# Fused attention and MoE on one core: the first MoE product of the last two token chunks by one level of Strassen's method, with the late attention replanned

## The chip, the core and the metric

The kernel runs on one core of one Trainium2 chip. The metric is device time in microseconds (us), the median of several runs of the whole program. The engines are TensorE (PE in the profile, PEld for its weight loads), VectorE (DVE), ScalarE (ACT), GpSimd (POOL) and SyncE (SP), which issues the DMAs. Each engine works through its own instructions in the order in which they were written, and waits on semaphores of the others.

## What is computed

Attention over q, k, v of 4 batches, 8 heads, 576 positions and 64 channels, in two parts that are added: one over the sequence averaged by 4, one over a band of seven neighbours. Its result is the input of a two-layer product with a gated activation:

```python
x = attn_out.transpose(0, 2, 1, 3).reshape(2304, 512)
h = x @ w_in                 # 2304 x 512 @ 512 x 2048
g = h * tanh(softplus(h))
out = g @ w_out              # 2304 x 2048 @ 2048 x 512
```

## The kernel before

**Precision.** TensorE works on fp32r operands, and each operand is kept as a high part (a copy rounded by ACT) and a low part (what is left, by a subtraction on DVE). Each product is three matmuls: high by high, high by low, low by high. So everything below that is multiplied exists twice, and one step is "x3" in the order.

**Tiling.** The 2304 tokens are six chunks of `CH` = 384. The 2048 hidden features are 16 tiles f of 128, the 512 channels four tiles p of 128. A slot s is one pair (chunk c, tile f): 96 slots, in the order chunks 0 and 1 interleaved, then chunks 2 to 5 one after another, 16 slots each. Slots 64 to 79 are chunk 4 and slots 80 to 95 chunk 5.

**A slot** (`slot`, L578 to L645) first makes h, transposed, as a 128x384 tile in a PSUM bank: four channel tiles by three matmuls of 384 columns, 12 matmuls (L591). Then comes the activation (L600 to L619): ACT exp (L605), DVE clamp and add (L606), ACT square, log and exp (L608, L609, L611), DVE product with h (L612, into the buffer mH), ACT copy of the high part (L615) and DVE low part (L617), both into g. Then g is multiplied by w_out: three blocks i of 128 tokens by three matmuls of 512 columns, 9 matmuls (L630), which add up over the 16 tiles f in three PSUM banks acc. After the chunk's last f, acc is copied out by ACT and DVE (L639, L642) and stored by SP (L645).

**Buffers.** PSUM has eight banks: two for h, three for acc of the current chunk, three (`att1`) for attention, which acc of chunk 1 borrows. In SBUF the buffers that matter here are mA (3), mH (2), g (2), stg (3 staging buffers of 128x1024, also for the outputs) and x (one tag for each channel tile, 3 buffers).

**Order.** Nothing runs in the order of the source. `op` records an instruction group with its engine, a cost, its buffers and a priority; `Plan.order` (L148) then plays the engines forward in time with the costs and latencies written in the file, and on each engine issues next what is ready and has the lowest priority number. That order is what the program gets; buffers of a tag are handed out in the order in which they were recorded. Priorities are slot numbers: a slot's first product has s, its activation s + 0.2, its second product s plus an entry of `LAG`, and attention of batch b and head pair p has `ATT[b][0] + ATT[b][1] * p + UNIT[b, p]`. Attention of batches 2 and 3 is spread between slots of chunks 2 and 3 this way, since chunk 4 needs batches 2 and 3, and chunk 5 batch 3.

Of the kernel before, what the change touches and what calls it, by code (L numbers as in the profile page):

```python
# [296 lines left out]
class Kernel:  # L297
# [48 lines left out]
    def attention(self, b, p, sb, ps, padded, loose):  # L346
# [25 lines left out]
        pc3 = lambda: pc()[:, :3 * C].rearrange("p (m c) -> p m c", m=3)  # L372
        cst, A = buf("cst", [P, 4, 3]), buf("A", [P, 3, C])
        cs = 2.0 ** -7
# [200 lines left out]
            self.w[nm, f] = w  # L575


    def slot(self, s, c, f):  # L578
# [20 lines left out]

        for c0, c1, key in parts:  # L600
            n, o_ = c1 - c0, slice(c0, c1)
            pl.prio = s + 0.2
# [9 lines left out]
            op("dve", dve(n), lambda o_=o_: nc.vector.scalar_tensor_tensor(  # L612
                out=H()[:, o_], in0=A()[:, o_], scalar=0.5, in1=h()[:, o_], op0=ALU.subtract, op1=ALU.mult),
               r=[h_, a_], w=[x_], two=False)
            op("act", act(n), lambda o_=o_: nc.scalar.activation(g()[:, 0, o_], H()[:, o_], AF.Copy, scale=-2.0),  # L615
               r=[x_], w=[one])
            op("dve", dve(n), lambda o_=o_: nc.vector.scalar_tensor_tensor(  # L617
                out=g()[:, 1, o_], in0=H()[:, o_], scalar=-2.0, in1=g()[:, 0, o_].bitcast(F32),
                op0=ALU.mult, op1=ALU.subtract), r=[x_, one], w=[two])  # L619
        wo = self.w["wo", f]  # L620
        if first:
            where, tag = ("attps", "att1") if c == 1 else ("moeps", None)
            self.acc[c] = [pl.buf(where, tag or f"acc{i}", [P, 512], F32, self.nb[where, tag] if tag else 1, f"acc{s}_{i}")
                           for i in range(3)]
        for i in range(3):
            a_ = self.acc[c][i]

            def mm2(i=i, a_=a_):
# [8 lines left out]
            o = pl.buf("stg", "stg", [P, 1024], F32, self.nstg, f"o{c}_{i}")  # L637
            if i % 2:
                op("dve", dve(512), lambda a_=a_, o=o: nc.vector.tensor_copy(o()[:, :512], a_()),  # L639
                   r=[a_], w=[o], prio=s + 1, two=False)  # L640
# [4 lines left out]
            op("sp", P * 2048 / RATE, lambda r0=r0, o=o: nc.sync.dma_start(self.out[r0:r0 + P, :], o()[:, :512]), r=[o], prio=s + 1)  # L645

    def run(self, ctx):
        tc = self.tc
# [42 lines left out]
        todo = [(c, f) for _, c, f in both] + [(c, f) for c in range(2, 6) for f in range(self.NF)]  # L691
# [94 lines left out]
```

## Time and profile before

| | |
|---|---|
| median of 3 runs | 526.4 us (525.13 to 528.31) |
| the profiled execution, its time | 523.15 us |
| its span in the trace | 521.4 us |
| PE busy | 504.4 us, 97% of the span, 4862 matmuls |
| ACT busy, DVE busy, POOL busy | 360.6, 299.0, 41.0 us |
| chain of waits | PE 73%, DVE 9%, ACT 7%, DMA 7% |

The span is the time from the first to the last instruction that the trace shows; what lies around it is 1.75 us in the profiled execution. Busy times are the time in which at least one instruction of the engine was under way, from its start to its end, so an engine whose instructions overlap at their ends is counted once. In the trace an instruction's duration is longer than its spacing from the next, where they follow each other without a wait.

### The profile page before, as it was taken

To read this page: it belongs to the slowest core of one execution; us is meant where nothing else is said; L and a number is where in the kernel's file an instruction comes from. 1 tells how busy PE (TensorE), PEld (TensorE's weight loads), DVE (VectorE), ACT (ScalarE), POOL (GpSimd) and SP (SyncE) were. 2 spreads that over 40 slices of the span, in tenths; PEclk is the share of its full clock that TensorE was granted. 3 is DMA by queue.
4 is the path that set the end of the run, shared out by engine and by line. 5 is a ranking of instruction groups with operands and counts; after the bars stand their busy time and mean duration, and the time that the engine had idled before them with its cause. 6 is when DMAs were issued, how large, how long until landed. Compare 5 with 4: busy or idle time off the path is not lost.

```text
span 521.4 us, 11714 instructions
## 1 busy us (share of the span) xinstructions
PE 504.4 (97%) x4862; PEld 432.5 (83%) x4862; DVE 299.0 (57%) x669; ACT 360.6 (69%) x872; POOL 41.0 (8%) x62
## 2 busy tenths in 40 slices
PE   8779989899999999999999999999999999999997
PEld 4556679798888999888888898899888989898885
DVE  5758999788884234576776745833333333334242
ACT  3668898899996567666666667666667565665753
POOL 6420112000000000001111110100000000000000
PEclk9979999999999999999999999999999999999999
DMA  8963476444530001233323313200001000010001
GB/s 345 411 235 117 142 263 215 161 161 159 206 123 0 1 0 62 107 126 122 116 97 138 127 61 108 93 1 1 1 0 62 0 1 1 1 61 1 0 1 60
DMA packets 11861, 50.66 MB, mean 97 GB/s; under 512 B 1312, under 2 KB 1312, under 8 KB 9760
## 3 DMA queue, kind: packets, MB, share of 16 engines
q1 hardware_dynamic: 11808, 49.91, 26.4%
q8 instruction: 38, 0.62, 0.5%
q14 instruction: 15, 0.12, 0.1%
HBM read 45.19 MB, written 4.72 MB: 96 GB/s over the span
## 4 chain that ended last, share of the span: by engine, by line
PE 73%; DVE 9%; ACT 7%; DMA 7%; issue 2%; SPq 0%; DVEq 0%
PE acc L630 31%; PE h L591 31%; DMA qk<-in_qk_dram 4%; DMA stg_wi<-in_w_in_dram 3%; PE sc L380 2%; PE sl L419 2%; PE pve L506 2%; DVE g L617 1%; DVE mH L612 1%; PE pvo L506 1%; PE pt L491 1%; DVE wo L573 1%; ACT mA L608 1%; PE warm L717 1%; ACT mA L609 1%
## 5 line engine op out<-in xcount | busy, mean ns | idle before, releaser
L591 PE MATMUL h<-x,wi 128*128 128x384 f32 x1152 | 226.0, 340 | 2.0 <-DVE mH L612 1.8
L630 PE MATMUL acc<-wo,g 128*128 128x512 f32 x864 | 219.0, 394 | 0.0
L591 PEld LDWEIGHTS h<-x,wi 128*128 128x128 f32 x1152 | 200.6, 188 | 17.5 <-DVE mH L612 9.5
L630 PEld LDWEIGHTS acc<-wo,g 128*128 128x128 f32 x864 | 159.8, 188 | 27.0 <-issue 0.2
L617 DVE SCALAR_TENSOR_TENSOR g<-mH,g 128x384 fp32r<-128x384 f32 (+1 forms) x98 | 55.5, 568 | 56.0 <-ACT g L615 55.5
L605 ACT ACTIVATE mA<-h 128x384 f32<-128x384 f32 (+1 forms) x98 | 47.0, 482 | 56.1 <-PE h L591 55.9
L612 DVE SCALAR_TENSOR_TENSOR mH<-mA,h 128x384 f32<-128x384 f32 (+1 forms) x98 | 53.1, 543 | 47.3 <-ACT mA L611 45.3
L606 DVE TENSOR_SCALAR mA<-mA 128x384 f32<-128x384 f32 (+1 forms) x98 | 34.9, 359 | 69.5 <-ACT mA L605 69.1
L615 ACT ACTIVATE g<-mH 128x384 fp32r<-128x384 f32 (+1 forms) x98 | 50.3, 515 | 25.3 <-PE acc L630 24.4
L608 ACT ACTIVATE mA<-mA 128x384 f32<-128x384 f32 (+1 forms) x98 | 50.5, 517 | 24.5 <-DVE mA L606 23.8
L609 ACT ACTIVATE mA<-mA,one 128x384 f32<-128x384 f32 (+1 forms) x98 | 59.5, 608 | 2.4
L611 ACT ACTIVATE mA<-mA 128x384 f32<-128x384 f32 (+1 forms) x98 | 49.9, 510 | 1.1
L452 POOL TENSOR_TENSOR vv<-vv 128x512 f32<-128x512 f32 x16 | 22.1, 1380 | 293.6 <-DMA vv<-in_vv_dram 293.6
L365 DVE TENSOR_REDUCE qkd<-qk 128x288 f32<-128x1152 f32 x16 | 21.5, 1346 | 11.3 <-DMA qk<-in_qk_dram 11.3
L506 PEld LDWEIGHTS pve<-PT,vv 38*64 38x64 f32 x640 | 20.8, 136 | 7.8 <-issue 4.5
L506 PE MATMUL pve<-PT,vv 38*64 38x32 f32 x640 | 22.8, 221 | 3.1 <-issue 3.0
L387 ACT ACTIVATE A<-sc,cst 128x144 f32<-128x144 f32 x48 | 17.9, 377 | 5.8 <-DVE cst L385 5.0
L419 PEld LDWEIGHTS sl<-qk 64*32 64x32 f32 x1152 | 12.4, 107 | 9.5 <-issue 6.5
L717 PE MATMUL warm<-ident 128*128 128x512 bf16 x61 | 18.6, 434 | 1.6 <-POOL ident masks.py:199 1.6
L419 PE MATMUL sl<-qk 64*32 64x38 f32 x1152 | 14.8, 198 | 4.1 <-issue 3.0
L531 ACT ACTIVATE x<-x 128x384 fp32r<-128x384 f32 (+1 forms) x32 | 12.8, 441 | 8.4 <-DVE x L519 8.0
L506 PE MATMUL pvo<-PT,vv 38*64 38x32 f32 x512 | 18.4, 222 | 0.2 <-ACT xd L486 0.2
(80 smaller groups left out, 421.7 us busy)
## 6 DMA issues: line engine op xcount, KB each, us to landing
vv<-in_vv_dram SPq DMA_DIRECT2D x16, 1152.0 KB, 5.3
qk<-in_qk_dram SPq DMA_DIRECT2D x16, 582.0 KB, 5.7
stg_wi<-in_w_in_dram SPq DMA_DIRECT2D x16, 512.0 KB, 4.1
stg_wo<-in_w_out_dram SPq DMA_DIRECT2D x16, 512.0 KB, 3.7
out_dram<-o SPq DMA_DIRECT2D x18, 256.0 KB, 2.0
```

The costliest lines, as they stand in the source:

```text
L419: nc.tensor.matmul(sl3()[64 * h + 32 * f:64 * h + 32 * f + 32, t], qk()[r_, 0, k0 + 3:k0 + 35], qk()[r_, 1, k0:k0 + KW], start=not pmask, ...
L506: nc.tensor.matmul(o_()[64 * h:64 * h + 64, c0:c0 + 32], vw()[64 * e:64 * e + KW, t // 2, f, 64 * h:64 * h + 64], PT()[64 * e:64 * e + KW, ...
L591: nc.tensor.matmul(h()[:, :CH], w()[:, a, kt * P:(kt + 1) * P], x()[:, b_, :], start=kt == 0 and j == 0, stop=kt == 3 and j == 2)
L605: op("act", act(n, True), lambda o_=o_: nc.scalar.activation(A()[:, o_], h()[:, o_], AF.Exp), r=[h_], w=[a_])
L606: op("dve", dve(n, True), lambda o_=o_: nc.vector.tensor_scalar(A()[:, o_], A()[:, o_], float(math.exp(20.0)), 1.0, op0=ALU.min, op1=ALU.a ...
L608: op("act", act(n), lambda o_=o_: nc.scalar.activation(A()[:, o_], A()[:, o_], AF.Square), w=[a_])
L609: op("act", act(n, False, 1), lambda o_=o_: nc.scalar.activation(A()[:, o_], A()[:, o_], AF.Ln, bias=self.one), w=[a_])
L611: op("act", act(n), lambda o_=o_: nc.scalar.activation(A()[:, o_], A()[:, o_], AF.Exp, scale=-1.0), w=[a_])
L612: op("dve", dve(n), lambda o_=o_: nc.vector.scalar_tensor_tensor(out=H()[:, o_], in0=A()[:, o_], scalar=0.5, in1=h()[:, o_], op0=ALU.subtr ...
L615: op("act", act(n), lambda o_=o_: nc.scalar.activation(g()[:, 0, o_], H()[:, o_], AF.Copy, scale=-2.0), r=[x_], w=[one])
L617: op("dve", dve(n), lambda o_=o_: nc.vector.scalar_tensor_tensor(out=g()[:, 1, o_], in0=H()[:, o_], scalar=-2.0, in1=g()[:, 0, o_].bitcast ...
L630: nc.tensor.matmul(a_(), g()[:, a, i * P:(i + 1) * P], wo()[:, b_], start=first and j == 0, stop=last and j == 2)
```

## The change

Chunks 4 and 5 are taken together, two f tiles at a time: a quartet of four slots (two chunks by two tiles). Their four products h are seen as a 2 by 2 matrix product of blocks: x split by channel halves (tiles 0 and 1, tiles 2 and 3) and by chunk, w_in by channel halves and by the two f tiles. Strassen's method in Winograd's form needs seven block products in place of eight. A block product is two channel tiles by three matmuls, so a quartet takes 42 matmuls of 384 columns in place of 48. The second products stay as they are.

- `prepare` makes the sums of x (S1 to S4, each for two channel tiles, with high and low parts) once, with priority 42. They lie in buffers that attention no longer uses (`vv`, `qk`), in x buffers, and work in the three stg buffers.
- `blocks` makes the sums of w_in (T1 to T4) for each pair of f tiles: 12 DVE instructions and 4 ACT copies of 128x256.
- `quartet` issues the products into the two h banks. One ACT copy takes the first product out of PSUM, and seven DVE additions (`plus`) combine the others into the four h tiles, now in SBUF; each tile then goes through the same activation (`tail`, the second half of the old `slot`).
- acc of chunk 5 takes the three attention banks, so both chunks add up at once. Outputs of chunk 4 go to x buffers, and outputs i = 0 and 1 of the other chunks share one stg buffer.
- `LAG` for the late slots is 9.95, was 7.07. `ATT` and `UNIT` of batches 2 and 3 change. Up to slot 47 the order of PE is the same as before.

```diff
-LAG = (7.26, 4.32, 7.07)
+LAG = (7.26, 4.32, 9.95)
...
-ATT = {0: (-817.1, 44.0), 1: (-77.2, 21.6), 2: (-43.4, 22.6), 3: (27.0, 12.1)}
+ATT = {0: (-817.1, 44.0), 1: (-77.2, 21.6), 2: (-49.7, 24.2), 3: (31.9, 8.4)}
...
+    def prepare(self):
...
+        pl.prio = SPRE
+        for j in range(2):
+            for k, x in (("a22", X(j + 2, 5)), ("a21", X(j, 5)), ("a11", X(j, 4)), ("a12", X(j + 2, 4))):
+                b, i, v = at(k, j)
+                op("dve", dve(W), lambda v=v, x=x: nc.vector.tensor_tensor(
+                    out=v(), in0=x()[:, 0].bitcast(F32), in1=x()[:, 1].bitcast(F32), op=ALU.add), r=[x], w=[(b, i)])
+            mix("a22", "a21", "a22", j, ALU.add)
+            mix("a21", "a11", "a21", j, ALU.subtract)
+            mix("a11", "a22", "a11", j, ALU.subtract)
+            mix("a12", "a12", "a11", j, ALU.subtract)
+            for k, t in (("a22", 1), ("a11", 2), ("a21", 3)):
+                split(k, j, t)
+        for j in range(2):
+            split("a12", j, 4)
...
+    def quartet(self, s, i):
...
+        def product(k, w, x):
+            bank = pl.buf("moeps", "h", [P, 512], F32, 2, f"h{k}_{s}")
+            wb_, wv = w
+            for j in range(2):
+                xb, key, xv = x[j]
+
+                def mm(j=j, xv=xv):
+                    for m, (a, b_) in enumerate(((0, 0), (0, 1), (1, 0))):
+                        nc.tensor.matmul(bank()[:, :CH], wv(a, j), xv()[:, b_], start=j == 0 and m == 0, stop=j == 1 and m == 2)
...
+        def plus(to, a, bank):
+            op("dve", dve(CH), lambda: nc.vector.tensor_tensor(
+                out=at[to](), in0=bank()[:, :CH], in1=at[a](), op=ALU.add),
+               r=[bank] + u[a] * (a != to), w=u[to], prio=s + UPRE, two=False)
+
+        bank = product(0, wt(w0, 0), xs(0, 4))
+        op("act", act(CH, True), lambda bank=bank: nc.scalar.activation(at["u1"](), bank()[:, :CH], AF.Copy),
+           r=[bank], w=u["u1"], prio=s + UPRE)
+        plus("u2", "u1", product(1, tt(2), ss(2)))
+        plus("u1", "u1", product(2, wt(w0, 2), xs(2, 4)))
+        self.tail(s, 4, 2 * i, u["u1"], at["u1"])
+        plus("u3", "u2", product(3, tt(3), ss(3)))
+        bank = product(4, tt(1), ss(1))
+        plus("u4", "u3", bank)
+        self.tail(s + 1, 5, 2 * i + 1, u["u4"], at["u4"], ("x", "x2"), False)
+        plus("u2", "u2", bank)
+        plus("u3", "u3", product(5, tt(4), xs(2, 5)))
+        self.tail(s + 2, 5, 2 * i, u["u3"], at["u3"], last=2 * i + 2 == self.NF)
+        plus("u2", "u2", product(6, wt(w1, 2), ss(4)))
+        self.tail(s + 3, 4, 2 * i + 1, u["u2"], at["u2"], ("x", "x3"))
...
-            where, tag = ("attps", "att1") if c == 1 else ("moeps", None)
+            where, tag = ("attps", "att1") if c in (1, 5) else ("moeps", None)
...
-        slots(todo[32:])
+        slots(todo[32:48])
+        self.prepare()
+        slots(todo[48:])
+        for i in range(self.NF // 2):
+            self.quartet(s, i)
+            s += 4
```

How the instructions move, at three places. In the names, h89 is the product of slot 89, h2_84 is block product 2 of the quartet that begins with slot 84, acc64 and acc65 are the sums of chunks 4 and 5, t2 and sfar are sums of w_in and x, and x3 at the end is a step's three matmuls.

PE, two slots late in the run, before (the rows of two slots, then the next acc):

```order
L591 MATMUL h89_5797<-x0_5_4058,wi9_1951 128x384 x3
L591 MATMUL h89_5797<-x1_5_4125,wi9_1951 128x384 x3
L591 MATMUL h89_5797<-x2_5_4524,wi9_1951 128x384 x3
L591 MATMUL h89_5797<-x3_5_4917,wi9_1951 128x384 x3
L591 MATMUL h90_5815<-x0_5_4058,wi10_2037 128x384 x3
L591 MATMUL h90_5815<-x1_5_4125,wi10_2037 128x384 x3
L591 MATMUL h90_5815<-x2_5_4524,wi10_2037 128x384 x3
L591 MATMUL h90_5815<-x3_5_4917,wi10_2037 128x384 x3
L630 MATMUL acc80_0_5642<-wo5_1728,g85_5785 128x512 x3
```

The same place in the quartet of slots 84 to 87, after:

```order
L678 MATMUL h2_84_5841<-x2_4_3517,wi10_2037 128x384 x3
L678 MATMUL h2_84_5841<-x3_4_3734,wi10_2037 128x384 x3
L678 MATMUL h3_84_5851<-x0_5_4056,t3_5_5706 128x384 x3
L678 MATMUL h3_84_5851<-x1_5_4123,t3_5_5706 128x384 x3
L678 MATMUL h4_84_5861<-sfar_4861,t1_5_5720 128x384 x6
L678 MATMUL h5_84_5873<-x2_5_4387,t4_5_5741 128x384 x3
L678 MATMUL h5_84_5873<-x3_5_4892,t4_5_5741 128x384 x3
L769 MATMUL acc65_0_5269<-wo6_1804,g78_5765 128x512 x3
L678 MATMUL h6_84_5896<-s4_0_5008,wi11_2077 128x384 x3
L769 MATMUL acc65_1_5304<-wo6_1804,g78_5765 128x512 x3
L769 MATMUL acc65_2_5313<-wo6_1804,g78_5765 128x512 x3
L678 MATMUL h6_84_5896<-s4_1_5013,wi11_2077 128x384 x3
```

A product that was 12 matmuls is now 6, four products follow each other without other work between them, and each still takes one of two banks.

DVE, what two slots issued before, in full:

```order
L606 TENSOR_SCALAR mA89_5819<-mA89_5819 128x384
L606 TENSOR_SCALAR mA90_5836<-mA90_5836 128x384
L617 SCALAR_TENSOR_TENSOR g87_5851<-mH87_5792,g87_5851 128x384
L612 SCALAR_TENSOR_TENSOR mH89_5858<-mA89_5819,h89_5797 128x384
L617 SCALAR_TENSOR_TENSOR g88_5867<-mH88_5810,g88_5867 128x384
L612 SCALAR_TENSOR_TENSOR mH90_5876<-mA90_5836,h90_5815 128x384
```

The first 11 of the 31 that a quartet issues now:

```order
L755 SCALAR_TENSOR_TENSOR g80_5828<-u1_80_5674,g80_5828 128x384
L685 TENSOR_TENSOR u23_84_5839<-h1_84_5792,u1_84_5834 128x384
L755 SCALAR_TENSOR_TENSOR g81_5845<-u4_80_5718,g81_5845 128x384
L685 TENSOR_TENSOR u1_84_5834<-h2_84_5841,u1_84_5834 128x384
L685 TENSOR_TENSOR u23_84_5839<-h3_84_5851,u23_84_5839 128x384
L744 TENSOR_SCALAR mA84_5859<-mA84_5859 128x384
L650 TENSOR_TENSOR t3_6_5866<-b12_6_5725,t3_6_5866 128x256
L685 TENSOR_TENSOR u4_84_5878<-h4_84_5861,u23_84_5839 128x384
L640 TENSOR_TENSOR b12_7_5885<-wi15_2323 128x256
L685 TENSOR_TENSOR u23_84_5839<-h4_84_5861,u23_84_5839 128x384
L685 TENSOR_TENSOR u23_84_5839<-h5_84_5873,u23_84_5839 128x384
```

The additions that free the banks stand between the sums of w_in for the next quartets and the activations of this one.

The entry into the first quartet: DVE before, at the end of chunk 3, and after.

```order
L617 SCALAR_TENSOR_TENSOR g63_5035<-mH63_4974,g63_5035 128x384
L612 SCALAR_TENSOR_TENSOR mH65_5042<-mA65_5003,h65_4980 128x384
L617 SCALAR_TENSOR_TENSOR g64_5051<-mH64_4994,g64_5051 128x384
L612 SCALAR_TENSOR_TENSOR mH66_5060<-mA66_5020,h66_4999 128x384
L606 TENSOR_SCALAR mA67_5069<-mA67_5069 128x384
L606 TENSOR_SCALAR mA68_5086<-mA68_5086 128x384
L639 COPY o3_1_5099<-acc48_1_4291 128x512
```

```order
L750 SCALAR_TENSOR_TENSOR mH63_5048<-mA63_5024,h63_4998 128x384
L755 SCALAR_TENSOR_TENSOR g63_5059<-mH63_5048,g63_5059 128x384
L650 TENSOR_TENSOR t2_1_5069<-b22_1_4973,t2_1_5069 128x256
L640 TENSOR_TENSOR b22_2_5075<-wi5_1710 128x256
L782 COPY o3_0_5092<-acc48_1_4480 128x512
L685 TENSOR_TENSOR u23_64_5101<-h1_64_5055,u1_64_5050 128x384
L685 TENSOR_TENSOR u1_64_5050<-h2_64_5065,u1_64_5050 128x384
```

PE there, after:

```order
L769 MATMUL acc48_0_4470<-wo15_2356,g63_5059 128x512 x3
L769 MATMUL acc48_1_4480<-wo15_2356,g63_5059 128x512 x3
L769 MATMUL acc48_2_4487<-wo15_2356,g63_5059 128x512 x3
L678 MATMUL h3_64_5105<-x0_5_4056,t3_0_4918 128x384 x3
L678 MATMUL h3_64_5105<-x1_5_4123,t3_0_4918 128x384 x3
```

The copy of the finished acc of chunk 3 now stands on DVE ahead of the addition that frees the bank which h3_64 needs.

## Rows read from the trace of the kernel before

**Rows 1.** The page, parts 1 and 2: PE busy, and its clock in 40 slices.
```profile
PE 504.4 (97%) x4862; PEld 432.5 (83%) x4862; DVE 299.0 (57%) x669; ACT 360.6 (69%) x872; POOL 41.0 (8%) x62
PEclk9979999999999999999999999999999999999999
```

**Rows 2.** The chain of waits in 425 to 446 us: start, duration, what.
```profile
430.13 4.21 PE h L591 x24
434.34 4.12 PE acc L630 x18
```

**Rows 3.** Stages: window, its length, busy time (instructions) of PE, PEld, DVE, ACT, POOL; clock.
```profile
60.00:120.00 60.00, 57.09 (x517) 50.10 (x516) 53.60 (x114) 53.13 (x120) 4.77 (x4) 1.00 0.55 185
240.00:320.00 80.00, 79.30 (x1064) 68.39 (x1063) 52.02 (x125) 55.24 (x147) 11.07 (x10) 1.00 0.32 115
320.00:390.00 70.00, 70.00 (x642) 62.15 (x642) 33.13 (x74) 45.56 (x100) 2.27 (x2) 1.00 0.08 27
390.00:507.00 117.00, 117.00 (x592) 105.07 (x591) 42.76 (x87) 73.16 (x144) 0.00 (x0) 1.00 0.04 14
```

**Rows 4.** What PE waited for in 60 to 120 us: us in total, times, longest.
```profile
PE h L591 <- DVE mH L612: 1.5, 2, 1.3
```

**Rows 5.** Groups by line and shape, 390 to 507 us: busy, mean ns; idle before.
```profile
L609 ACT ACTIVATE mA<-mA,one 128x384 f32<-128x384 f32 x28 | 17.2, 616 | 0.8
L612 DVE SCALAR_TENSOR_TENSOR mH<-mA,h 128x384 f32<-128x384 f32 x29 | 16.0, 553 | 1.0
L617 DVE SCALAR_TENSOR_TENSOR g<-mH,g 128x384 fp32r<-128x384 f32 x28 | 15.7, 559 | 33.3 <-ACT g L615 33.0
L608 ACT ACTIVATE mA<-mA 128x384 f32<-128x384 f32 x28 | 14.7, 525 | 6.2 <-DVE mA L606 6.0
L605 ACT ACTIVATE mA<-h 128x384 f32<-128x384 f32 x28 | 13.8, 492 | 23.9 <-PE h L591 23.9
L606 DVE TENSOR_SCALAR mA<-mA 128x384 f32<-128x384 f32 x28 | 10.1, 360 | 38.9 <-ACT mA L605 38.9
```

**Rows 6.** Groups of DVE by line and shape, whole run.
```profile
L519 DVE TENSOR_TENSOR x<-pvo,xd 128x256 f32<-128x256 f32 x16 | 6.6, 415 | 0.0
L639 DVE COPY o<-acc 128x512 f32<-128x512 f32 x6 | 4.2, 692 | 4.9 <-PE acc L630 4.9
```

**Rows 7.** Timeline of DVE at 69 and 103 us: start, duration, instruction.
```profile
69.10 0.41 DVE L519 TENSOR_TENSOR x<-pvo,xd 128x256 f32<-128x256 f32 x1
69.43 0.55 DVE L617 SCALAR_TENSOR_TENSOR g<-mH,g 128x384 fp32r<-128x384 f32 x1
...
102.73 0.35 DVE L606 TENSOR_SCALAR mA<-mA 128x384 f32<-128x384 f32 x1
103.00 0.55 DVE L617 SCALAR_TENSOR_TENSOR g<-mH,g 128x384 fp32r<-128x384 f32 x1
103.46 0.55 DVE L612 SCALAR_TENSOR_TENSOR mH<-mA,h 128x384 f32<-128x384 f32 x1
```

**Rows 8.** Timeline of PE while DVE is at its busiest.
```profile
87.31 4.35 PE L591 MATMUL h<-x,wi 128*128 128x384 f32 x24
91.51 4.28 PE L630 MATMUL acc<-wo,g 128*128 128x512 f32 x18
...
104.07 2.37 PE L591 MATMUL h<-x,wi 128*128 128x384 f32 x12 [1.33 <-DVE mH L612]
```

**Rows 9.** Timeline of all engines, 432 to 434 us.
```profile
432.30 0.49 ACT L605 ACTIVATE mA<-h 128x384 f32<-128x384 f32 x1 [1.60 <-PE h L591]
432.82 0.36 DVE L606 TENSOR_SCALAR mA<-mA 128x384 f32<-128x384 f32 x1 [0.95 <-ACT mA L605]
433.22 0.53 ACT L608 ACTIVATE mA<-mA 128x384 f32<-128x384 f32 x1 [0.43 <-DVE mA L606]
```

**Rows 10.** Timeline, the end of the run.
```profile
507.17 10.40 PE L630 MATMUL acc<-wo,g 128*128 128x512 f32 x45
517.61 0.60 ACT L642 ACTIVATE o<-acc 128x512 f32<-128x512 f32 x1 [0.76 <-PE acc L630]
```

More of the change, by code (lines that the diff above doesn't have):

```diff
@@ L41 @@
 TAIL = 0
+SPRE = 42
+TPRE = -2
+UPRE = -2
 TICK, BUSY, PACE = 3413.3, 3060, 1.6
@@ new lines, in blocks @@
+    def blocks(self, i):
+        nc, pl = self.nc, self.plan
+        op, n = pl.op, 256
+        w0, w1 = self.w["wi", 2 * i], self.w["wi", 2 * i + 1]
+        t = {k: pl.buf("att", tag, [P, n], F32, 1, f"{k}_{i}")
+             for k, tag in (("b11", "A"), ("b12", "AT"), ("b21", "vd"), ("b22", "qkd"))}
+        for k, w, c in (("b11", w0, 0), ("b12", w1, 0), ("b22", w1, n), ("b21", w0, n)):
+            op("dve", dve(n), lambda k=k, w=w, c=c: nc.vector.tensor_tensor(
+                out=t[k](), in0=w()[:, 0, c:c + n].bitcast(F32), in1=w()[:, 1, c:c + n].bitcast(F32), op=ALU.add),
+               r=[w], w=[t[k]])
+        T = {}
+        for j, (ko, a, b_, place) in ((1, ("b11", "b12", "b11", ("att", "L"))), (3, ("b12", "b22", "b12", ("att", "x32"))),
+                                      (2, ("b22", "b22", "b11", ("att", "PT"))), (4, ("b21", "b21", "b22", ("stg", "tmp")))):
+            op("dve", dve(n), lambda ko=ko, a=a, b_=b_: nc.vector.tensor_tensor(
+                out=t[ko](), in0=t[a](), in1=t[b_](), op=ALU.subtract), r=[t[a], t[b_]], w=[t[ko]])
+            T[j] = w = pl.buf(*place, [P, 2, n], F32R, 1, f"t{j}_{i}")
+            op("act", act(n), lambda w=w, ko=ko: nc.scalar.activation(w()[:, 0], t[ko](), AF.Copy), r=[t[ko]], w=[(w, 0)])
+            op("dve", dve(n), lambda w=w, ko=ko: nc.vector.tensor_tensor(
+                out=w()[:, 1], in0=t[ko](), in1=w()[:, 0].bitcast(F32), op=ALU.subtract), r=[t[ko], (w, 0)], w=[(w, 1)])
+        return T
@@ L594, in slot, with tail @@
             op("pe", 527, mm, r=[w, x], w=[h], cols=1152, prio=s + 0.1 * kt / 4)
-        A = pl.buf("mish", "mA", [P, CH], F32, NMISH[0], f"mA{s}")
-        H = pl.buf("mish", "mH", [P, CH], F32, NMISH[1], f"mH{s}")
-        g = pl.buf("mish", "g", [P, 2, CH], F32R, 2, f"g{s}")
+        self.tail(s, c, f, h)
+    def tail(self, s, c, f, h, own=None, place=("mish", "g"), last=None):
+        nc, pl = self.nc, self.plan
+        op = pl.op
+        last = f == self.NF - 1 if last is None else last
+        A = pl.buf("mish", "mA", [P, CH], F32, NMISH[0], f"mA{s}")
+        psum = own is None
+        if psum:
+            Hv, own = pl.buf("mish", "mH", [P, CH], F32, NMISH[1], f"mH{s}"), h
+            h, H = [[(b, m) for m in range(3)] for b in (h, Hv)]
+        else:
+            Hv, H = own, h
+        g = pl.buf(*place, [P, 2, CH], F32R, 3 if place[0] == "x" else 2, f"g{s}")
         parts = [(0, CH, None)] if s < 95 - TAIL else [(i * P, (i + 1) * P, i) for i in range(3)]
@@ L612, in slot @@
             op("dve", dve(n), lambda o_=o_: nc.vector.scalar_tensor_tensor(
[L613 to L616, printed above, removed]
+                out=Hv()[:, o_], in0=A()[:, o_], scalar=0.5, in1=own()[:, o_], op0=ALU.subtract, op1=ALU.mult),
+               r=[*h_, a_], w=x_, two=not psum)
+            op("act", act(n), lambda o_=o_: nc.scalar.activation(g()[:, 0, o_], Hv()[:, o_], AF.Copy, scale=-2.0),
+               r=x_, w=[one])
             op("dve", dve(n), lambda o_=o_: nc.vector.scalar_tensor_tensor(
-                out=g()[:, 1, o_], in0=H()[:, o_], scalar=-2.0, in1=g()[:, 0, o_].bitcast(F32),
-                op0=ALU.mult, op1=ALU.subtract), r=[x_, one], w=[two])
+                out=g()[:, 1, o_], in0=Hv()[:, o_], scalar=-2.0, in1=g()[:, 0, o_].bitcast(F32),
+                op0=ALU.mult, op1=ALU.subtract), r=[*x_, one], w=[two])
         wo = self.w["wo", f]
+        first = c not in self.acc
         if first:
-            where, tag = ("attps", "att1") if c == 1 else ("moeps", None)
+            where, tag = ("attps", "att1") if c in (1, 5) else ("moeps", None)
             self.acc[c] = [pl.buf(where, tag or f"acc{i}", [P, 512], F32, self.nb[where, tag] if tag else 1, f"acc{s}_{i}")
@@ L626, in slot, with mm2 @@
             a_ = self.acc[c][i]
-            def mm2(i=i, a_=a_):
+            def mm2(i=i, a_=a_, first=first, last=last):
                 for j, (a, b_) in enumerate(((0, 0), (0, 1), (1, 0))):
@@ L690, in run @@
         both = sorted([(f, 0, f) for f in range(self.NF)] + [(f + LEAD + 0.5, 1, f) for f in range(self.NF)])
-        todo = [(c, f) for _, c, f in both] + [(c, f) for c in range(2, 6) for f in range(self.NF)]
+        todo = [(c, f) for _, c, f in both] + [(c, f) for c in range(2, 4) for f in range(self.NF)]
         s = 0
```

71 lines of the change are left out of this document (61 added, 10 removed).

## The prediction

> **What bounds the kernel now.** I read the page first, then the chain of waits, then stages in a table of windows, and then single spacings. The page has PE busy for 97% of the span at full granted clock after the first slices [rows 1], and busy PE can still hide gaps, so the chain decides. In the last stage it is PE alone: 24 matmuls of the first product, then 18 of the second, and so on, with no other engine between them [rows 2]. That gives two prices: 4.21 / 24 = 0.1754 us for a matmul of 384 columns, 4.12 / 18 = 0.2289 us for one of 512. The stages show the same: from 320 us on PE is never idle, with DVE at 47% and then 37% and ACT at 65% and 63%; only early, with DVE busy 53.6 of 60 us, does PE lose 2.9 us [rows 3]. So in slots 64 to 95 the time is the number of matmuls, and the other engines have room. The question is how much of that room the change uses up.
>
> **What is removed.** Eight quartets lose 6 matmuls each of 384 columns: 48 x 0.1754 = 8.4 us, all on the chain. The order shows six matmuls for each product in place of twelve, and seven products. The price holds when DVE is busy: at 87 us, where DVE is at 89%, 24 matmuls take 91.51 - 87.31 = 4.20 us [rows 3, 8]. (The Trainium skill, "TensorE: Matmul & The Clock Gate", Back-to-back issue gap, gives columns / 2.4 + 2.5 ns, 162.5 ns here, by which the gain would be 7.8 us. The trace disagrees, with 175.4 ns, and the trace is used.)
>
> **What is added, quartet by quartet.** PE needs 42 x 0.1754 + 36 x 0.2289 = 15.6 us for a quartet, before it was 16.7. DVE issues 31 instructions: seven additions and eight activation steps of 384 elements, four clamps, 12 sums of 256. Where they follow each other the spacing is 0.46, 0.27 and 0.33 us [rows 7], so 15 x 0.46 + 4 x 0.27 + 12 x 0.33 = 12.0 us, 77% of 15.6. An addition from PSUM is priced as L612, which reads PSUM and SBUF too [rows 5]. ACT has four times five activations (four at 0.525, the log at 0.616), one copy from PSUM at 0.492 and four copies of 256, for which 0.525 is an upper bound: at most 13.5 us, 86% [rows 5]. Neither is full, so the sums of w_in and x cost nothing by themselves; they are hidden behind PE. What counts is whether PE waits for them in turn. Three waits are new in each quartet.
>
> First, a bank. A product lasts 6 x 0.1754 = 1.05 us, and the one after the next needs its bank. The release takes the step from PE to the reader, one addition, and the step back: 0.06 (the twelfth matmul from 430.13 ends at 432.24, ACT starts at 432.30 [rows 2, 9]), 0.55, and 0.06 (DVE ends at 104.01, PE starts at 104.07 [rows 7, 8]), together 0.67. That fits, if DVE is at the addition when the product ends; in the order the additions of h2 and h3 follow at most one other instruction. The bank of h4 needs two additions, 0.46 more, 1.13; there a step of acc (0.69) beside h5 (1.05) covers it.
>
> Second, the buffer mH. The h tiles u1 and u4 hold both of its buffers, so the copy of h0 into the next u1 waits for the low part g of the old u1, nearly a whole quartet of DVE work later, and h2 of the next quartet waits for that copy. From one h2 to the next: 1.05 for the product, 0.06, 29 of the 31 DVE instructions (11.1), 0.04 + 0.49 for the copy, 0.06: 12.8 us. Going through the order with the same prices, DVE waits inside this for h3 (0.6), for the square, log and exp of slot s + 3 (0.9) and for small steps (0.2): 14.5 us against 15.6. So it fits with 1.1 to spare, and I take nothing for quartets four to eight; the bounds are 0 and the share that PE loses in the stage with DVE at 89%, 4.9% of 78 us = 3.8 us [rows 3].
>
> Third, acc of chunk 5 needs the attention banks, so attention has to be over by then; in the order the last unit is through PE in slot 60, and the first acc65 comes over 30 us of PE work later. That costs nothing.
>
> **The entry.** Here work piles up: the last attention results, half of `prepare`, two sets of `blocks` and the activations of slots 60 to 63. From the last attention matmul to h2 of the fourth quartet the order has 180 matmuls of 384 and 120 of 512, 59 us, against 137 DVE instructions, 54 us by their spacing. The nearest rows are those of 60 to 120 us, with the same load: PE lost 2.9 us there, 1.5 of it waiting for L612 [rows 3, 4]. So the entry is bounded by 0 and 2.9. Place by place: the copy of acc48_1 stands before the first addition. It starts 0.06 after that acc, takes 0.60 before the next instruction (0.69 in full [rows 6], less the overlap of 0.09), and the addition and the step back bring h3_64 to 0.6 us after the end of acc48_2. h6_64 waits for two additions with t3 and b12 in front, 1.4 against 1.05, so 0.3. mH60 comes after 21 instructions (8.9 us, with its own 0.55 and 0.06 9.5) against 9.3 us of PE work, so 0.2. The chain of slot 63 (0.49, 0.36, 0.53, 0.62, 0.53, 0.55 and 0.2 of steps, with one other copy of 0.53 on ACT) is 3.8 us, as long as PE's work before h1_64, so with any delay 0.3. h2_68 waits for u1, 0.3. Together **1.7 us**.
>
> **Attention moved.** Two units of batch 3 go through PE a few slots earlier and closer together. Their loads on SP and sums on POOL keep their places in those queues; only output stores stand elsewhere. Three units in the same rhythm, 240 to 320 us, cost PE 0.7 us idle [rows 3], 0.23 each. Bounds 0 and 0.7, I take 0.3. `prepare` and two sets of `blocks` put 24 x 0.46 + 24 x 0.33 = 19 us of DVE into a stage where it is busy 33 of 70 [rows 3]; its cover is PE work.
>
> **The end.** PE stops at 517.57, 3.8 us before the span ends, for a copy and a store [rows 10]. That is the same after. Before, 45 matmuls after the last h hid the last activation; after, 81 do, with one addition more in the chain. Nothing.
>
> **Sum.** -8.4 + 1.7 + 0.3 = -6.4 us. The profiled execution would go from 523.15 to 516.8 (span 515.0). The median of the runs is 3.25 above that execution, so the forecast for the median is 526.4 - 6.4 = **520.0 us**. With the bounds of entry and attention, -8.4 to -4.8: 518.0 to 521.6; the upper bound of the later quartets is the second rival.
>
> **The rivals.**
>
> *All of it.* The steps between engines are shorter than I add them up, and entry and attention hide everything: 526.4 - 8.4 = 518.0. For it: PE is never idle from 320 us on. Against: the copy before the first addition is a wait on any prices. Chance 0.12.
>
> *The room goes.* DVE is as full as in 60 to 120 us throughout, since additions, sums and activations wait for each other in one line, and PE loses 4.9% of all eight quartets: 8 x 15.6 x 0.049 = 6.1, with attention -8.4 + 6.1 + 0.3 = -2.0, or 524.4, no change that can be told. For it: two banks, and three products in a row that each need an addition in time. Against: 77% is not 89%, and part of the 2.9 us belonged to other waits [rows 4]. Chance 0.19.
>
> *DVE sets the pace.* If DVE instructions did not overlap at their ends, each would hold the engine for its whole duration: 0.55 for 0.46, 0.415 for 0.33, 0.36 for 0.27 [rows 5 to 7]. The loop through mH then grows by 29 x 0.09 = 2.6 to 17.1 us, longer than the old 16.7. Eight quartets lose 3.8 in place of gaining 8.4, and with entry and attention the time is 526.4 + 3.8 + 2.0 = 532.2. It decides from a loop of 16.4 us on. The same comes about if the overlap is lost only in this order, where many instructions need the one just before. (The Trainium skill, "VectorE: DVE Perf Modes", The TRN2 errata — SBUF-src ops pay a fixed extra latency per instruction, says that SBUF latency is exposed between instructions, and has (N + 151) / 0.96 ns for an fp32 add: 557 for 384 and 424 for 256. By that rule this rival holds.) Against it: 103.00 to 103.46 is 0.46 us for an instruction of 0.55 [rows 7]. Chance 0.11.
>
> That the change doesn't remove what it says is excluded by the order.
>
> **How the numbers follow.** The forecast has 0.58. Half a per cent, 2.6 us, is about what a measurement of this kernel can tell from no change. Faster by more than that: the forecast and the first rival, 0.70. Within it: the second, 0.19. Slower: the third, 0.11. The range reaches from the first rival, less 1.2 for the spread of the runs below their median (525.13), to the second, plus 1.1: 516.8 to 525.5. It leaves out the third rival and the edges.
>
> **What would show it.** Right: 336 matmuls of first products late in the run, at 0.175 us each, quartets of 15.6 us from the fourth on, PE idle some 2 us between the last attention and the third quartet, most of it just after the last acc of chunk 3, and additions spaced 0.46 us. Wrong: PE waiting for additions or for the u1 copy in every quartet, or a quartet of over 16 us; then DVE's line, and not the matmul count, sets the time. A slower first half would mean that attention's new places cost more than counted.

## The result, and the profile after

The changed kernel took **519.6 us** (median of 4 runs, 518.83 to 520.38) where the kernel before took 525.8 beside it: a ratio of 0.987, 95% interval 0.984 to 0.991. In two later sets of runs, on two different chips, the ratio was 0.989 (0.986 to 0.993) both times, 519.7 against 525.3 us and 518.5 against 524.3. So the change is faster by 5.6 to 6.2 us in medians. The forecast of 520.0 held. What it says of the parts is another matter, since one term was too small and one was too large.

The page of the changed kernel, parts 1, 4 and 5 (busy time; the chain that ended last by engine; the group of the new additions):

```profile
PE 497.3 (96%) x4814; PEld 425.2 (82%) x4814; DVE 366.5 (71%) x845; ACT 372.4 (72%) x920; POOL 40.5 (8%) x62
...
PE 60%; DVE 19%; ACT 9%; DMA 8%; issue 2%; POOL 0%; SPq 0%; DVEq 0%; POOLq 0%; ACTq 0%
...
L685 DVE TENSOR_TENSOR u<-h,u 128x384 f32<-128x384 f32 x56 | 30.2, 552 | 5.0 <-PE h L678 2.6
```

48 matmuls are gone and PE is busy for 7.1 us less [rows 1], but PE's share of the chain has fallen from 73% to 60% and DVE's has grown from 9% to 19%: PE is no longer the only one that sets the time. Where that is, the windows say (the same stages as in [rows 3], columns as there):

```profile
240.00:320.00 80.00, 77.42 (x1271) 66.09 (x1271) 58.59 (x141) 53.28 (x150) 11.25 (x11) 1.00 0.35 128
320.00:390.00 70.00, 68.58 (x412) 60.27 (x410) 43.67 (x100) 46.00 (x97) 1.91 (x2) 1.00 0.04 13
390.00:507.00 117.00, 116.39 (x580) 104.14 (x581) 94.00 (x232) 88.17 (x205) 0.00 (x0) 1.00 0.02 7
```

Before, PE had no idle time at all from 320 us on. Now it idles for 1.4 us in 320 to 390 and 0.6 after. (The 2.6 us of idle in the first row lie ahead of 298 us, where the order of PE is the old one and executions, those of the experiments below included, idle for 0.7 to 2.7 us.) DVE is at 80% of the last stage, where I had 77%, and ACT at 75%, under my bound of 86%. The chain of waits in that stage (start, duration, what) shows the steady quartets:

```profile
440.62 4.18 PE h L678 x24
...
456.25 4.17 PE h L678 x24
...
471.88 4.18 PE h L678 x24
...
487.51 4.18 PE h L678 x24
...
494.83 18.42 PE acc L769 x81
```

From 440.62 to 456.25, 471.88 and 487.51 it is 15.63 us each time, PE alone; the prediction had 15.6 [rows 2]. The time that was given back lies ahead of that, in PE's timeline (start, duration, matmuls; in brackets PE's idle time before and its releaser):

```profile
330.66 2.27 PE L717 MATMUL h<-x,wi 128*128 128x384 f32 x12
333.11 0.79 PE L717 MATMUL h<-x,wi 128*128 128x384 f32 x3 [0.17 <-DVE mH L750]
...
368.62 4.28 PE L769 MATMUL acc<-wo,g 128*128 128x512 f32 x18
373.78 2.35 PE L717 MATMUL h<-x,wi 128*128 128x384 f32 x12 [0.88 <-DVE mH L750]
...
380.83 1.21 PE L678 MATMUL h<-x,wi 128*128 128x384 f32 x6
...
385.35 4.28 PE L769 MATMUL acc<-wo,g 128*128 128x512 f32 x18
390.20 1.33 PE L678 MATMUL h<-x,t 128*128 128x384 f32 x6 [0.57 <-DVE u L685]
...
392.40 1.22 PE L678 MATMUL h<-x,t 128*128 128x384 f32 x6
393.93 1.32 PE L678 MATMUL h<-s,wi 128*128 128x384 f32 x6 [0.31 <-DVE u L685]
...
426.17 1.21 PE L678 MATMUL h<-x,t 128*128 128x384 f32 x6
427.48 1.31 PE L678 MATMUL h<-sfar,t 128*128 128x384 f32 x6
```

The loss at each place is more than the idle time in brackets. At 390.20: 18 matmuls of 0.2289 us from 385.35 on make room for the next product at 389.47, so it is 0.73 late, not 0.57. The idle time is counted from the end of the last matmul, which under full load overlaps its successor. Then the six matmuls take 1.33 us, where six without a wait take 1.21 (380.83): 0.11 more. So h3_64 cost 0.84. In the same way h62 (373.78) cost 1.04 + 0.10 = 1.14, h6_64 (393.93) 0.48 + 0.11 = 0.59, h4 of the third quartet (427.48) 0.26 + 0.10 = 0.36, and h54 (333.11) 0.35 + 0.1 = 0.45. That is 3.4 us.

**A stretch to compare by.** The first 300 us differ by some 4 us from execution to execution, with the same order of PE. Both orders have the same PE work up to a block of nine matmuls that begins with slot 47's first products and follows the scores of batch 3's third unit (in the expectations below I call these "the last attention scores", wrongly: the fourth unit's come later). From there to the end of the last matmul the trace gives the same length again to about 0.15 us. For the kernel before the block is this row; its last matmul ends at 517.57 [rows 10], 219.65 us later:

```profile
297.92 1.83 PE L591 MATMUL h<-x,wi 128*128 128x384 f32 x9
```

For the changed kernel the same two rows of PE's timeline give 494.67 + 18.56 - 298.85 = **214.38 us**, 5.27 less:

```profile
298.85 1.83 PE L717 MATMUL h<-x,wi 128*128 128x384 f32 x9
...
494.67 18.56 PE L769 MATMUL acc<-wo,g 128*128 128x512 f32 x81
```

The repeats (e0 and e10 below) gave 214.43 and 214.28.

### The profile page after: what moved, and what is told of

Read it like the earlier page. It is cut to its first block, busy times and chain, and to the rows that moved or that the text cites. A ratio compares the mean times of both kernels' runs of the same rounds, so it can differ in the third digit from the quotient of the medians.

```text
span 517.1 us, 11888 instructions
## 1 busy us (share of the span) xinstructions
PE 497.3 (96%) x4814; PEld 425.2 (82%) x4814; DVE 366.5 (71%) x845; ACT 372.4 (72%) x920; POOL 40.5 (8%) x62
## 4 chain that ended last, share of the span: by engine, by line
PE 60%; DVE 19%; ACT 9%; DMA 8%; issue 2%; POOL 0%; SPq 0%; DVEq 0%; POOLq 0%; ACTq 0%
PE acc L769 26%; PE h L717 16%; PE h L678 8%; DMA qk<-in_qk_dram 5%; PE pve L509 2%; PE sc L383 2%; DVE u L685 2%; DVE g L755 2%; DMA stg_wi<-in_w_in_dram 2%; PE sl L422 1%; DVE mA L744 1%; ACT mA L747 1%; PE pt L494 1%; ACT mA L746 1%; DMA vv<-in_vv_dram 1%
## 5 line engine op out<-in xcount | busy, mean ns | idle before, releaser
L717 PE MATMUL h<-x,wi 128*128 128x384 f32 x768 | 155.3, 341 | 3.1 <-DVE mH L750 3.0
L717 PEld LDWEIGHTS h<-x,wi 128*128 128x128 f32 x768 | 134.1, 188 | 15.7 <-DVE mH L750 8.6
L750 DVE SCALAR_TENSOR_TENSOR mH<-mA,h 128x384 f32<-128x384 f32 x64 | 35.2, 550 | 44.2 <-ACT mA L749 43.4
L743 ACT ACTIVATE mA<-h 128x384 f32<-128x384 f32 x64 | 31.1, 486 | 22.3 <-PE h L717 22.1
L755 DVE SCALAR_TENSOR_TENSOR g<-mH,g 128x384 fp32r<-128x384 f32 x64 | 37.1, 580 | 13.8 <-ACT g L753 13.5
L753 ACT ACTIVATE g<-mH 128x384 fp32r<-128x384 f32 x64 | 33.3, 520 | 12.5 <-PE acc L769 7.4
L685 DVE TENSOR_TENSOR u<-h,u 128x384 f32<-128x384 f32 x56 | 30.2, 552 | 5.0 <-PE h L678 2.6
L368 DVE TENSOR_REDUCE qkd<-qk 128x288 f32<-128x1152 f32 x16 | 21.5, 1346 | 11.8 <-DMA qk<-in_qk_dram 11.8
L509 PEld LDWEIGHTS pve<-PT,vv 38*64 38x64 f32 x640 | 21.5, 140 | 5.7 <-ACT PT L501 2.6
L753 ACT ACTIVATE g<-u 128x384 fp32r<-128x384 f32 (+1 forms) x34 | 16.7, 498 | 10.4 <-PE acc L769 9.5
L755 DVE SCALAR_TENSOR_TENSOR g<-u,g 128x384 fp32r<-128x384 f32 (+1 forms) x34 | 17.7, 529 | 9.0 <-ACT g L753 9.0
L750 DVE SCALAR_TENSOR_TENSOR u<-mA,u 128x384 f32<-128x384 f32 (+1 forms) x34 | 17.8, 529 | 5.0 <-ACT mA L749 4.8
```

What stands on the lines that cost most here:

```text
L509: nc.tensor.matmul(o_()[64 * h:64 * h + 64, c0:c0 + 32], vw()[64 * e:64 * e + KW, t // 2, f, 64 * h:64 * h + 64], PT()[64 * e:64 * e + KW, ...
L685: op("dve", dve(CH), lambda: nc.vector.tensor_tensor(out=at[to](), in0=bank()[:, :CH], in1=at[a](), op=ALU.add), r=[bank] + u[a] * (a != t ...
L743: op("act", act(n, psum), lambda o_=o_: nc.scalar.activation(A()[:, o_], own()[:, o_], AF.Exp), r=h_, w=[a_])
```

## The experiments

The theory: the quartets pay their 8.4 us in full, and some 3 us go back at a few waits where the new work begins, each caused by what stands ahead in DVE's list. Rivals: the matmuls are worth less than 8.4; the new attention plan costs it; DVE's load costs PE time in every quartet. Each edit makes the planner draw up the whole order anew, so in e3, e6, e8 and e9 PE's order moves along with the edit, though only ahead of 431 us.

**The change again (e0).** No edit.

> The changed kernel once more, on another chip. Forecast of record: 6.4 us less than before; rival 'The room goes': about 2 us less; rival 'All of it': 8.4 less. The first pair gave 526 to 519.6, so I expect 5.5 to 7.0 less, and in the trace a steady quartet of 15.6 us with no wait of PE for an addition after the third quartet.

Measured: 519.7 against 525.3 us, ratio 0.989 (0.986 to 0.993). The waits stand at the same places with the same lengths (1.04, 0.73 and 0.50 us late at h62, h3_64 and h6_64), so they belong to the order and not to chance.

**Fewer matmuls alone (e1).** In `slot` of the kernel before:

```diff
+            m = 2 if s >= 64 and (kt == 3 or kt == 2 and s % 2) else 3
...
-                for j, (a, b_) in enumerate(((0, 0), (0, 1), (1, 0))):
+                for j, (a, b_) in enumerate(((0, 0), (0, 1), (1, 0))[:m]):
```

> The kernel before, with 48 matmuls of 384 columns left out and nothing added: from slot 64 on the product of low w and high x is left out for the last quarter of the channels in every slot and for the third quarter in every odd slot (so the output lacks those terms). The attention's places are the old ones. If a matmul costs 0.1754 us wherever it stands (my term), the time falls by 8.4 us, to about 517.4, since nothing new is waited for; then the change gives back some 2 us by its entry. If late matmuls are partly hidden (PE's busy time counts something else), the fall is 6.5 or less, and the change's own waits cost next to nothing.

Measured: 516.1 us, 9.2 less, ratio 0.982 (0.979 to 0.985). In the stretch, from PE's timeline:

```profile
299.54 1.83 PE L592 MATMUL h<-x,wi 128*128 128x384 f32 x9
...
500.59 10.40 PE L631 MATMUL acc<-wo,g 128*128 128x512 f32 x45
```

500.59 + 10.40 - 299.54 = 211.45, which is 8.20 less than before, 0.171 us for each of 48 matmuls. The term of 8.4 holds within 0.2. The change's 5.3 is 2.9 short of that.

**Attention alone (e2).** The kernel before with the two tables of the change:

```diff
-ATT = {0: (-817.1, 44.0), 1: (-77.2, 21.6), 2: (-43.4, 22.6), 3: (27.0, 12.1)}
+ATT = {0: (-817.1, 44.0), 1: (-77.2, 21.6), 2: (-49.7, 24.2), 3: (31.9, 8.4)}
```

(and `UNIT` likewise.)

> The kernel before with the attention plan of the change alone (its places and unit shifts), first products as before. My term: +0.3 us (bounds 0 and 0.7), about 526. Rival: the earlier attention costs more, +1 us or over, and then most of the difference between 8.4 and the measured gain lies there and not at the entry of the new products.

Measured: 524.0 against 525.3 us, ratio 0.998 (0.995 to 1.000), and in the stretch:

```profile
300.27 1.83 PE L591 MATMUL h<-x,wi 128*128 128x384 f32 x9
...
509.49 10.40 PE L630 MATMUL acc<-wo,g 128*128 128x512 f32 x45
```

519.89 - 300.27 = 219.62 against 219.65: nothing. Neither my 0.3 nor the rival's 1 us is there. The 1.3 us by which the medians differ would have to lie before the stretch; they are at the edge of the interval.

**Sums made once (e3).** In `quartet` of the changed kernel:

```diff
-        T = self.blocks(i)
+        T = self.T = self.blocks(i) if i == 0 else self.T
```

> The changed kernel with the sums of x and w_in that feed the products made for the first quartet only and used again in the other seven (so seven quartets compute with wrong sums): 12 instructions of DVE and 4 of ACT fewer per quartet, 4.0 and 2.1 us. My theory: the sums are hidden behind PE, so the steady quartet stays 15.6 us, and only the entry (the second and third quartet) gets easier: 0.3 to 1.0 us less than the changed kernel. Rivals 'The room goes' and 'DVE sets the pace': DVE's load costs PE time in every quartet, so 3 us or more less.

Measured: 517.2 us, 2.5 less than e0 beside it, but the stretch says where:

```profile
296.66 1.83 PE L717 MATMUL h<-x,wi 128*128 128x384 f32 x9
...
491.83 18.56 PE L769 MATMUL acc<-wo,g 128*128 128x512 f32 x81
```

510.39 - 296.66 = 213.73, 0.65 less than with the change, inside 0.3 to 1.0; PE's timeline has it at the entry, where h62, h6_64 and h4 of the third quartet are less late. (This execution reached the stretch 2.2 us earlier than the changed kernel's.) The chain of waits has the quartet's start at 469.04 and 484.67, 15.63 us as before. So a third of DVE's list, taken out of every steady quartet, is worth nothing there: the rivals *The room goes* and *DVE sets the pace* fall.

**The buffer's turn (e6).** `two` is the staging buffer of u2 and u3. Buffers of a tag are handed out in the order in which they were recorded, so the first quartet's was the one that the output copy of acc48_1 fills. In the edit it is recorded ahead of the outputs:

```diff
+        self.two = pl.buf("stg", "stg", [P, 1024], F32, self.nstg, "u23_64")
...
-        two = pl.buf("stg", "stg", [P, 1024], F32, self.nstg, f"u23_{s}")
+        two = self.two if i == 0 else pl.buf("stg", "stg", [P, 1024], F32, self.nstg, f"u23_{s}")
```

> The changed kernel, with the buffer of u2 and u3 of the first quartet taken one turn earlier in its ring, so that the first addition (u23_64 <- h1_64) no longer has to wait for the copy of acc48_1; the accumulations of slots 62 and 63 then stand behind the first products of the quartet. My theory: the wait of 0.73 us before h3_64 (0.84 with the slow first matmul after it) is this copy, so 0.6 to 0.9 us less than the changed kernel: 213.5 to 213.8 us from the last attention scores (batch 3, first matmul of x after them, near 299 us) to the last matmul, where the changed kernel has 214.4. Rival: the additions are late for another reason (the chain of slot 63), and the wait moves to the next product: no change, 214.4.

The wait in question, in DVE's timeline of the changed kernel: the copy of acc48_1, then the additions.

```profile
388.99 0.69 DVE L782 COPY o<-acc 128x512 f32<-128x512 f32 x1 [3.15 <-PE acc L769]
389.60 1.14 DVE L685 TENSOR_TENSOR u<-h,u 128x384 f32<-128x384 f32 x2
```

Measured in the stretch of e6:

```profile
299.59 1.83 PE L717 MATMUL h<-x,wi 128*128 128x384 f32 x9
...
494.54 18.56 PE L769 MATMUL acc<-wo,g 128*128 128x512 f32 x81
```

213.51 us, 0.87 less, as expected. (Median 518.5 against 524.4, ratio 0.989, 0.985 to 0.992: with no changed kernel beside it, too coarse for this.) Freed of the copy, the 18 matmuls of the last second products (385.35 above) now stand behind the next products of the quartet on PE, so the edit moves PE's order together with the buffer. The waits at h3_64, h6_64 and h4 of the third quartet are all gone, which is 1.8 us, but between 399 and 425 us some small ones of about 0.2 each are new, 1.0 us in all.

**mH60 first (e8).** `prepare`'s sums of x get a later priority:

```diff
-SPRE = 42
+SPRE = 60.3
```

> The changed kernel with the sums of x planned at 60.3 in place of 42, so that on VectorE the multiplication mH60 stands two instructions after g59's neighbour and not behind eight more sums. My theory: PE's wait of 1.03 us before h62 (1.14 with the slow matmul behind it) is these eight sums, since ScalarE had mH60's input ready some 4 us earlier, so this wait goes and the stretch from the last attention scores to the last matmul falls from 214.4 to 213.2 to 213.5. Rival: the sums are needed anyway, and the lost time comes back at h64 or h1_64, where their results are read: 214.2 to 214.6.

In the changed kernel ACT hands over what mH60 needs at 369.0 (first row), but DVE comes to mH60 (last row) at 373.18, behind g59 and seven sums of x (columns: start, duration, instruction):

```profile
368.51 0.51 ACT L749 ACTIVATE mA<-mA 128x384 f32<-128x384 f32 x1
```

```profile
363.96 0.48 DVE L522 TENSOR_TENSOR x<-pve,xd 128x320 f32<-128x320 f32 x1
...
369.18 0.55 DVE L755 SCALAR_TENSOR_TENSOR g<-mH,g 128x384 fp32r<-128x384 f32 x1
369.64 0.55 DVE L614 TENSOR_TENSOR sy<-sy,sy 128x384 f32<-128x384 f32 x1
370.23 0.56 DVE L614 TENSOR_TENSOR sy<-sy 128x384 f32<-128x384 f32 x1
...
372.71 0.55 DVE L609 TENSOR_TENSOR x<-sy,x 128x384 fp32r<-128x384 f32 x1
373.18 0.55 DVE L750 SCALAR_TENSOR_TENSOR mH<-mA,h 128x384 f32<-128x384 f32 x1
```

Measured in the stretch of e8:

```profile
298.62 1.83 PE L717 MATMUL h<-x,wi 128*128 128x384 f32 x9
...
493.14 18.56 PE L769 MATMUL acc<-wo,g 128*128 128x512 f32 x81
```

493.14 + 18.56 - 298.62 = 213.08 us, 1.30 less, somewhat more than expected. PE waits for no mH any more. The wait at h54 is gone with the one at h62: at slot 51 the first of these sums stood ahead of an mH and of the next slot's clamp on DVE (329.67 and 330.13 us with the change, 326.85 and 328.38 in e8), which ACT and then h54 waited for. The other waits stand as they were (0.73 and 0.50 us late). The rival, that the sums are missed later, is not seen. (Median 519.4 against 524.4, ratio 0.990, 0.986 to 0.993: again the stretch decides.)

**Both (e9, and e11 beside the changed kernel, e10).** e6 and e8 together.

> Both edits of the two runs before together. If both waits were order and nothing more, the two add up: 212.2 to 212.7 us from the last attention scores to the last matmul (214.4 now), and some 2 us less than the changed kernel in time. If VectorE lacks time at the entry as a whole, the waits move to other products and the sum of the two is not reached: 213.2 or more.

> The changed kernel again, as the partner of the next run on the same chip. Expected: 6 us less than the kernel before (5 to 7), 214.4 us from the last attention scores to the last matmul.

> The changed kernel with both edits (the buffer's turn, and the sums of x at 60.3) again, beside the changed kernel on one chip. From the first time (211.11 us from the last attention scores to the last matmul, 3.3 us less than the changed kernel, with no wait of PE left) I expect 3 to 4 us less than the changed kernel and 8.5 to 9.5 less than the kernel before. Rival: the two waits come back with other run-to-run shifts of the early stages, 1 to 2 us less than the changed kernel.

PE's timeline of e9:

```profile
299.83 1.83 PE L717 MATMUL h<-x,wi 128*128 128x384 f32 x9
...
492.38 18.56 PE L769 MATMUL acc<-wo,g 128*128 128x512 f32 x81
```

and its windows:

```profile
320.00:390.00 70.00, 70.00 (x426) 62.80 (x426) 47.02 (x111) 49.32 (x104) 2.42 (x2) 1.00 0.03 12
390.00:507.00 117.00, 117.00 (x582) 104.58 (x581) 90.82 (x224) 85.62 (x199) 0.00 (x0) 1.00 0.02 8
```

211.11 us: 8.54 less than before, 3.27 less than the change, and PE has no idle time from 320 us on. In time e9 took 515.8 us, ratio 0.983 (0.980 to 0.987). e11 gave 211.10 us in the stretch and **515.5 us** in time, ratio 0.984 (0.980 to 0.989), beside e10 with 518.5 and the kernel before with 524.3 on the same chip: 3.0 less than the change. The two edits together give more than their sum (0.87 + 1.30 = 2.17), because the small waits that e6 alone brought are gone too. Why they are is not shown. So all that the change gave back, it gave back for the order on DVE and the turn of one buffer, with the places on PE that go with them. This version beats both kernels.

**More work on DVE (e5, e12).** In `blocks`, values unchanged (e12 has `four * 6`):

```diff
-        for k, w, c in (("b11", w0, 0), ("b12", w1, 0), ("b22", w1, n), ("b21", w0, n)):
+        four = (("b11", w0, 0), ("b12", w1, 0), ("b22", w1, n), ("b21", w0, n))
+        for k, w, c in four + four * 3:
```

> The changed kernel with the four sums of w_in at the head of each quartet's list made four times over (12 more additions of 256 elements per quartet on VectorE, 4.0 us; the values are the same). By my spacings VectorE then needs 16.0 us for a quartet and PE 15.6, and the loop through mH 14.5 + 4.0 = 18.5. If the loop counts, a quartet takes about 18.5 us and the time rises by some 20 us; if only VectorE's own load counts, 16.0 to 16.5 us and 3 to 7 us more; if spare time on VectorE were far larger than I reckon, nothing changes (under 1 us more).

Measured: 520.3 us, ratio 0.993 (0.991 to 0.996), and in the stretch 503.52 + 13.80 - 300.59 = 216.73 us, 2.35 more than the change: less than the 3 to 7 us expected, though the quartets came out as expected. The copies of the first product (ACT's timeline) mark the quartets:

```profile
425.00 0.47 ACT L691 ACTIVATE u<-h 128x384 f32<-128x384 f32 x1
...
490.21 0.47 ACT L691 ACTIVATE u<-h 128x384 f32<-128x384 f32 x1
```

Four quartets in 65.21 us, 16.3 each, and DVE is busy for 113.4 of the 117 us from 390 on (94.0 with the change). So DVE's load counts, not a loop of 18.5. Over half of the 2.35 us is at the entry (1.81 us late at h3_64, 0.83 at h6_64, where it was 0.73 and 0.50); in the steady quartets PE lived mostly from the lead it had, since it is busy for 64.8 of the 65 us from 425 to 490. A loop through mH was not what limited this kernel; but the planner put the extra sums where DVE had room, so the length of the loop in the changed kernel's own order was not tested.

> The changed kernel with the four sums of w_in at the head of each quartet's list made seven times over (24 more additions of 256 elements per quartet; the values are the same). Now VectorE must be the bound, and the length of a quartet tells what its instructions cost when nothing else limits. By spacings (0.46, 0.27, 0.33 us): 15 x 0.46 + 4 x 0.27 + 36 x 0.33 = 19.9 us a quartet, some 30 to 36 us more in all than the changed kernel. By whole durations without overlap (0.55, 0.36, 0.415), as the rival 'DVE sets the pace' had it: 24.6 us a quartet, some 65 to 75 us more.

Measured: 550.1 us, 31.7 more than e10 beside it, inside the 30 to 36 of the spacings and far from 65 to 75. ACT's timeline of e12:

```profile
475.87 0.49 ACT L691 ACTIVATE u<-h 128x384 f32<-128x384 f32 x1
...
496.51 0.47 ACT L691 ACTIVATE u<-h 128x384 f32<-128x384 f32 x1
...
516.67 0.49 ACT L691 ACTIVATE u<-h 128x384 f32<-128x384 f32 x1
```

20.6 and 20.2 us for a quartet (21.5 and 21.0 before those), with DVE busy for 116.3 of the 117 us from 390 on. Its timeline shows the spacing:

```profile
456.78 4.77 DVE L641 TENSOR_TENSOR b<-wi 128x256 f32<-128x256 f32 x14
461.48 1.33 DVE L647 TENSOR_TENSOR b<-b,b 128x256 f32<-128x256 f32 x3
```

14 sums of 0.415 us follow each other in 461.48 - 456.78 = 4.70 us, 0.336 each. Whole durations would make 24.6. So DVE's instructions do overlap at their ends when DVE is the bound, and that rival falls in its premise too. (The Trainium skill, "VectorE: DVE Perf Modes", The TRN2 errata, has (N + 151) / 0.96 ns for an fp32 add, by estimate 557 ns for 384 elements and 424 for 256, which agrees with the durations here, 550 and 415. The prediction's rival took this as what one costs in a row, and 14 sums would then need 5.9 us. The trace has 4.70: here it is the duration of one addition and not the spacing.)

## Why the prediction was right, and where it was off

- **Removed, -8.4.** Right: 8.20 alone (e1), 8.54 where nothing is waited for (e9).
- **The quartets.** Right: 15.63 us from the fourth on, and 12 more or fewer sums on DVE change the steady state little (e3, e5). Quartets four to eight cost 0, the lower bound of that term; the share of 4.9% that was carried over from 60 to 120 us [rows 3, 4] didn't appear.
- **The loop through mH, 14.5 of 15.6.** It fitted, as said. That it would set the pace with more on DVE was wrong for e5.
- **The entry, 1.7.** This term was too small: 2.9 (1.14 at h62, 0.84 at h3_64, 0.59 at h6_64, 0.36 at h4 of the third quartet), at the upper bound of 2.9. The step that failed is the one for mH60. It set 9.5 us of DVE work against 9.3 us of PE work as if both began together, 0.2. The instruction that opens DVE's list began at 363.96, PE's products after the last attention matmul at 363.27, so 0.69 was missing; and DVE needed 9.22 us for the 21 instructions, not 8.9, since a sum of x that overwrites an operand of the sum just ahead of it starts only 0.04 us after that one's end, so the two follow at 0.59 us (369.64, 370.23) and not at 0.46. PE's side was 9.47, so 0.69 + 9.22 + 0.60 - 9.47 = 1.04. For h3_64 the mechanism was right: the copy, 0.61, then the addition and the step back, 390.20 as worked out; but its price was 0.84 and not 0.6, because I counted the idle time between two matmuls and not how late the next one starts, nor the slower first matmul. The same holds for h6_64, with 0.31 idle as worked out and a price of 0.59. The wait at h4 of the third quartet was not in the working at all. The 0.3 each for h1_64 and h2_68 were not there.
- **Attention moved, 0.3.** Wrong: 0 (e2). The wait that stands in that stage, 0.45 at h54, is made by `prepare`'s first sums (e8), which I had called covered by PE.
- **The end, 0.** Right: 81 matmuls behind the last product hid it.
- **The sum.** -8.4 + 2.9 + 0.45 = -5.0, against -5.27 in the stretch; the medians, -5.6 to -6.2, lie nearer the forecast's -6.4 than the stretch does, and the difference of 0.3 to 0.9 must lie in the first 300 us, where the two kernels have the same PE order, or in the scatter of the medians, since the span ends 3.8 us after the last matmul in both. That part was luck. So the forecast was some 1 us better than its working deserved.
- **The rivals.** *The room goes* and *DVE sets the pace* are refuted by e3, e5 and e12. (The sum of *DVE sets the pace* is 0.2 us too high: eight quartets at 17.1 in place of 15.6 are 12.0 us, less 8.4 is 3.6 and not 3.8.) *All of it* was wrong of this kernel, but e9 shows that it could be had: what spoke against it, the copy before the first addition, was no wait "on any prices" but a matter of which buffer was handed out.

## What to carry to other kernels

When a change trades matmuls for work on another engine, a steady state with room there need not pay for it, and here it did not; look at the place where the new work begins, and there at when each engine can start, not only at how much each has to do. A wait that stands at the same place in every execution, for an instruction whose inputs were ready 4 us before, is an order to be changed: two small edits of the order were worth 3 us here, over half of what the large change had gained. Price a wait by how late the next matmul starts against its usual spacing, since idle time leaves out the overlap.

## What the runs showed of the hardware

- After a wait, the first product took 0.10 to 0.12 us longer for its six matmuls (1.33 against 1.21), at every such place in the changed kernel, so many short waits cost more than their length.
- In e12 PE's granted clock, at 1.00 in all the late stages of the changed kernel, fell in the middle of three quartets. Its windows of 430 to 450 us (columns as in [rows 3]) and its timeline, with an addition of DVE's as the last row:

```profile
430.00:435.00 5.00, 5.00 (x26) 4.38 (x26) 5.00 (x14) 3.91 (x9) 0.00 (x0) 1.00 0.00 2
...
440.00:445.00 5.00, 2.46 (x8) 2.40 (x9) 4.66 (x15) 2.84 (x7) 0.00 (x0) 0.70 0.00 0
```

```profile
442.54 1.33 PE L679 MATMUL h<-sfar,t 128*128 128x384 f32 x3 [2.92 <-ACT t L650]
443.66 1.16 PE L679 MATMUL h<-snear,t 128*128 128x384 f32 x3
...
444.86 0.56 DVE L686 TENSOR_TENSOR u<-h,u 128x384 f32<-128x384 f32 x1 [0.28 <-PE h L679]
```

PE had waited for 2.92 us; the three matmuls after that took 1.33 us where three take 0.69 at the full clock. The granted clock is 0.50 from 442.1 to 445.4 us, the lower of its two levels, 1.2 GHz. DVE was the bound there and waited only 0.28 us for the slowed product, so little of it shows in the time there. The waits of up to 0.9 us in the changed kernel left the clock at 1.00, and so did two of 2.09 and 2.17 us in e12 (at 422 and 463 us).
